# Attention of a three-stage kernel with channels on the partitions, fp32 products, and the triangular solve over pairs of chunks in PSUM

## Chip, cores and metric

The kernel runs on one core of one Trainium2 chip. The metric is device microseconds of one launch of the whole kernel.

## What is computed

The output of a linear attention with a decaying state goes through a top-1 mixture of experts and then through a gated MLP. The attention is the part that the change touches:

```
B, H, S, D = 4, 8, 768, 40
for t in range(S):
    kt, vt, rt = (k[:, :, t], v[:, :, t], r[:, :, t])
    wt, at, bt = (w[:, :, t], a[:, :, t], b[:, :, t])
    y[:, :, t] = np.einsum('bhd,bhde->bhe', rt, state)
    Sa = np.einsum('bhde,bhe->bhd', state, at)
    state_decay = state * wt[:, :, None, :] - np.einsum('bhd,bhe->bhde', Sa, bt)
    state = state_decay + np.einsum('bhd,bhe->bhde', vt, kt)
x = y in rows of tokens, 3072 x 320
# experts: of the tokens with x @ w_skip > 0, each through its best of 8 experts
out[tokens] = x + gate * (relu(x @ w1[e]) @ w2[e])
# second MLP, d_ff = 2048
h = x @ w_in; g = h * sigmoid(1.702 * h); result = g @ w_out
```

All inputs and outputs are float32.

## The kernel before

**Stages.** Attention works in 12 chunks of 64 tokens, all 32 heads at a time. The router's logits follow each half of a chunk's output; then come routing, the eight experts in groups of at most 240 tokens, and the second MLP in 6 blocks of 512 tokens. The first loads and casts of the MLPs' weights run beside attention.

**One chunk of attention.** Tokens lie on the partitions when the chunk is loaded (two batches of 64). The method `g_prep` takes the running products of the decays w by two scans on VectorE (L244, L256), one in each direction from the middle of a half chunk, and has TensorE transpose them (L269). `g_a` and `g_kb` multiply a, k and b with them on POOL (L303, L340), split the fp32 results into an fp16 high part and an fp16 rest (ScalarE's cast, POOL's subtraction), and have the DMA queue of SP transpose the parts. `g_scale` moves decays from chunk to chunk by 160 small fp32 matmuls (L204).

`g_gram` takes the products of a with k and b inside 32-token blocks (L373), transposes them into the tile Z (L385) and inverts the triangular blocks: the matrix starts as ones on the diagonal in the SBUF tile Tm, and 31 steps of two VectorE instructions follow, L396 (a column of Tm by a row of Z into tmp) and L399 (tmp added to Tm):

```
tmp[:, :n * st]   = Tm[:, r0:, st] * Z3[:, st, 0:st]        # L396, SBUF and SBUF
Tm[:, r0:, 0:st]  = Tm[:, r0:, 0:st] + tmp                  # L399, SBUF and SBUF
```

The inverse is split into fp16 parts and taken by four DMAs into the block-diagonal tile te. `g_ag` and `g_ab` make the masked products of a with k (L434, L440; fp16 rest by POOL at L451) and of a with b (L472, L480). `g_chain` solves for u of a chunk, half the heads at a time: it gathers the right side in PSUM (slots gx0, gx1), multiplies by te (L593), by the a-b products and by te again, with each vector split into parts at L585; an identity matmul (L589) takes the part that was cast out of the PSUM sum. Then it updates the state (L648 and on) and splits that. `g_sn`, `g_vt` and `g_r` bring the state, u and r into the other orientation by DMA. `g_pq` (L738, mask at L741) and `g_post` (L763 and L766, with L772) make the output; L763 is an fp32 product, of two column halves one after the other.

**Order.** Each method is a generator that yields its steps with planned costs. `weave` merges them: the step that can start first by the planned times of the engines goes next, with due times from the list RANK. What comes out is a fixed order for each engine's queue. PSUM has slots: 3 of kind c, 3 of kind g, two for gx; a step that wants one waits for it. `g_warm` puts filler matmuls (L792) on TensorE where its plan has gaps, 840 of them.

Of the kernel before, what the change touches and what calls it, by code (L numbers as in the profile page):

```python
# [23 lines left out]
def host_attn(r, k, v, w, a, b):  # L24
    B, H_, S, D_ = r.shape
    NC = S // L

    def nat(z):
        return z.reshape(2, 2, H, NC, L, D).transpose(3, 1, 4, 0, 2, 5).reshape(NC, 128, 640)

    def five(z):
        return z.reshape(2, 2, H, NC, L, D)

    k5, b5 = five(k), five(b)
    kb = np.empty((NC, 2, L, 2, 2, H, D), np.float32)
# [69 lines left out]
class Attn(Flow):  # L105
# [14 lines left out]
    def __init__(self, tc, ctx, args, NC, emit_x):  # L120
# [49 lines left out]
        for t in [st0] + self.S:  # L170
            nc.gpsimd.memset(t, 0.0)
# [1548 lines left out]
```

## Time and profile before

| | |
|---|---|
| median of 3 runs | 1163.12 us (1162.36 to 1168.79) |
| span of the profiled execution | 1164.9 us |
| busy: TensorE, VectorE | 929.5 us (80%), 797.7 us (68%) |
| busy: ScalarE, POOL | 497.2 us (43%), 473.1 us (41%) |
| mean granted TensorE clock | 0.833 of full speed |
| DMA | 140 MB in 301,625 packets |

The busy times are of one profiled execution, over all its stages; they don't say which engine ends a stage. The granted clock has two levels, 1.0 (2.4 GHz) and 0.5 (1.2 GHz); a mean between them is a mixture. A row `out<-in` names the tile that is written and those that are read, and the number after x is a count.

### The profile page before, as it was taken

What the parts mean: (1) busy time and instruction counts of PE and PEld (TensorE: products, weight loads), DVE (VectorE), ACT (ScalarE), POOL (GpSimd) and SP (SyncE); (2) the same over time, 40 slices, a digit from 0 to 9 for tenths busy, and PEclk for the clock granted to TensorE, in tenths of its full rate; (3) what the DMA queues carried; (4) which work ended last, traced back from release to release, by engine and by line L of the source; (5) the groups of instructions that cost most, each with busy time, mean ns of one, the idle gap of its engine ahead of it and who ended that gap; (6) DMA issues with size and microseconds to landing.
All of it is one profiled execution on the core that took longest, in us unless ns stands there. A gap on an engine that the chain in (4) does not pass through costs nothing.

```text
span 1164.9 us, 27321 instructions
## 1 busy us (share of the span) xinstructions
PE 929.5 (80%) x11343; PEld 654.4 (56%) x11343; DVE 797.7 (68%) x1655; ACT 497.2 (43%) x987; POOL 473.1 (41%) x405
## 2 busy tenths in 40 slices
PE   5757788598787877968840298995979999999998
PEld 5647667486566675756640176672335555555556
DVE  6599999999999999988658986766972111121110
ACT  2324555445544545436424456442543332333330
POOL 4343345435455544445313635442443332333330
PEclk8776777776777786689855599997989999999999
DMA  6564589799889798865796687434300101010000
GB/s 174 138 152 81 102 169 180 166 160 169 194 154 175 147 186 136 187 111 107 132 258 176 225 192 214 152 130 113 94 26 12 28 22 37 12 29 13 12 12 31
DMA packets 301625, 140.08 MB, mean 120 GB/s; under 512 B 271652, under 2 KB 284712, under 8 KB 299432
## 3 DMA queue, kind: packets, MB, share of 16 engines
q1 hardware_dynamic: 299192, 133.91, 52.8%
q0 software_dynamic: 2304, 4.36, 1.3%
q8 instruction: 91, 1.49, 0.5%
q14 instruction: 38, 0.31, 0.1%
HBM read 62.18 MB, written 14.48 MB: 66 GB/s over the span
## 4 chain that ended last, share of the span: by engine, by line
DVE 37%; PE 37%; DMA 11%; issue 7%; POOL 3%; ACT 3%; SPq 2%; POOLq 0%; DVEq 0%; ACTq 0%
DVE tmp L396 8%; DVE Tm L399 8%; PE c L1552 5%; PE c L1553 4%; PE c L1554 4%; PE g L1512 4%; PE g L1515 3%; PE gx L1512 3%; DMA w2s<-w 3%; PE gx L1515 2%; PE g L763 2%; PE gx L792 2%; DVE pq L741 2%; DMA d_s<-wia 1%; DMA g_x<-xd,g_ig 1%
## 5 line engine op out<-in xcount | busy, mean ns | idle before, releaser
L1535 POOL TENSOR_TENSOR glo<-g,ghi 128x512 f16<-128x512 f32 x96 | 113.8, 1187 | 221.9 <-ACT ghi L1534 221.8
L396 DVE SCALAR_TENSOR_TENSOR tmp<-Tm,Z 128x78 f32<-128x78 f32 (+21 forms) x372 | 148.9, 410 | 8.6 <-ACT Tm L383 3.0
L399 DVE TENSOR_TENSOR Tm<-Tm,tmp 128x78 f32<-128x78 f32 (+21 forms) x372 | 146.7, 405 | 5.1
L792 PE MATMUL gx<-c 128*128 128x192 f16 x840 | 131.6, 300 | 6.4 <-DMA c<-c 3.5
L1531 DVE SCALAR_TENSOR_TENSOR g<-g,sg 128x512 f32<-128x512 f32 x57 | 39.2, 688 | 133.3 <-ACT sg L1529 133.3
L1552 PE MATMUL c<-wo_hi,ghi 128*128 128x320 f16 x384 | 115.9, 302 | 5.9 <-ACT wo_hi L1457 5.9
L1553 PE MATMUL c<-wo_lo,ghi 128*128 128x320 f16 x384 | 115.1, 300 | 0.9 <-DVE wo_lo L1460 0.9
L1554 PE MATMUL c<-wo_hi,glo 128*128 128x320 f16 x384 | 115.2, 300 | 0.0
L792 PEld LDWEIGHTS <-c 128*128 128x128 f16 x840 | 82.0, 116 | 39.5 <-issue 30.1
L1534 ACT CAST ghi<-g 128x512 f16<-128x512 f32 x96 | 59.2, 618 | 76.1 <-DVE g L1531 76.1
L1531 DVE SCALAR_TENSOR_TENSOR g<-gx,sg 128x512 f32<-128x512 f32 x39 | 26.9, 689 | 89.9 <-ACT sg L1529 89.9
L451 POOL TENSOR_TENSOR gkl<-m,gkh 64x512 f16<-64x512 f32 x48 | 58.5, 1218 | 58.7 <-ACT gkh L449 46.4
L1512 PEld LDWEIGHTS <-wi_hi 128*128 128x128 f16 x480 | 45.6, 99 | 60.2 <-DMA xt<-xe 13.3
L763 PE MATMUL g<-km,pq 128*64 128x40 f32 x768 | 58.1, 261 | 26.2 <-DVE pq L741 26.1
L1512 PE MATMUL g<-xt,wi_hi 128*128 128x512 f16 x285 | 71.5, 382 | 1.3 <-DVE g L1531 1.3
L763 PEld LDWEIGHTS g<-km,pq 128*64 128x64 f32 x768 | 54.9, 172 | 29.4 <-DVE pq L741 28.4
L1515 PEld LDWEIGHTS <-wi_lo 128*128 128x128 f16 (+1 forms) x288 | 27.8, 97 | 64.1 <-issue 41.6
L1529 ACT ACTIVATE sg<-g 128x512 f32<-128x512 f32 x57 | 33.7, 595 | 64.2 <-PE g L1515 64.2
L1198 POOL TENSOR_TENSOR w2l<-w2s,w2h 128x1280 f16<-128x1280 f32 x16 | 42.9, 2687 | 44.2 <-ACT w2h L1196 44.0
L1512 PE MATMUL gx<-xt,wi_hi 128*128 128x512 f16 x195 | 49.6, 386 | 12.9 <-DMA xt<-xe 12.9
L1552 PEld LDWEIGHTS <-ghi 128*128 128x128 f16 x384 | 37.5, 98 | 28.6 <-issue 16.1
L1515 PE MATMUL g<-xt,wi_lo 128*128 128x512 f16 x171 | 52.1, 382 | 0.0
(215 smaller groups left out, 2340.6 us busy)
## 6 DMA issues: line engine op xcount, KB each, us to landing
w2s<-w SPq DMA_DIRECT2D x8, 1280.0 KB, 8.6
w1s<-w1a SPq DMA_DIRECT2D x8, 1024.0 KB, 9.4
km<-raw SPq DMA_DIRECT2D x12, 640.0 KB, 4.7
wt<-wt SPq DMA_DIRECT2D x11, 640.0 KB, 5.7
d_s<-wo SPq DMA_DIRECT2D x10, 512.0 KB, 3.6
d_s<-wia SPq DMA_DIRECT2D x8, 512.0 KB, 4.7
v<-rv SPq DMA_DIRECT2D x12, 320.0 KB, 4.2
am<-raw SPq DMA_DIRECT2D x12, 320.0 KB, 5.5
```

Of the source, the lines that this page charges most:

```text
L396: nc.vector.scalar_tensor_tensor(out=tv, in0=Tm[:, r0:, st:st + 1].to_broadcast([128, n, st]), scalar=-2.0 ** -18, in1=Z3[:, st:st + 1, 0: ...
L399: nc.vector.tensor_tensor(out=Tm[:, r0:, 0:st], in0=Tm[:, r0:, 0:st], in1=tv, op=ALU.add)
L763: mm(d, lhsT=self.pq[:, q], rhs=km[:, 40 * p:40 * p + 40], start=h == 0, stop=False, **kw)
L792: self.nc.tensor.matmul(self.X[:, 320:], lhsT=self.C['c_i'][:, 0], rhs=self.C['c_rep'].rearrange('p a b -> p (a b)')[:, :192], start=first ...
L1512: nc.tensor.matmul(h, lhsT=self.whi[:, k % 3, fs], rhs=xt[:, k], start=k == 0, stop=False)
L1515: nc.tensor.matmul(h, lhsT=self.wlo[:p, k, fs], rhs=xt[:p, k], start=False, stop=k == 2)
L1531: nc.vector.scalar_tensor_tensor(out=g, in0=h, scalar=2.0 ** -6, in1=sg2, op0=ALU.mult, op1=ALU.mult)
L1534: nc.scalar.copy(out=ghi[:, f], in_=g)
L1535: nc.gpsimd.tensor_tensor(out=glo[:, f], in0=g, in1=ghi[:, f], op=ALU.subtract)
L1552: nc.tensor.matmul(o, lhsT=ghi[:, f, s], rhs=self.ohi[:, f], start=f == 0, stop=False)
L1553: nc.tensor.matmul(o, lhsT=ghi[:, f, s], rhs=self.olo[:, f], start=False, stop=False)
L1554: nc.tensor.matmul(o, lhsT=glo[:, f, s], rhs=self.ohi[:, f], start=False, stop=f == 15)
```

## The change

**Layout.** The host lays out a, k, b, r and the decays with channels on the partitions, 40 of each 64 partitions for one half of the batch. The scans run on 128 x 1024 tiles, and a, k and b are multiplied in place by POOL; the results go straight into matmuls. A new `g_f` has TensorE transpose the decays that the output needs, and `g_kb` the products with k and b (tile km).

**Products.** All of attention's matmuls are fp32. The fp16 parts with their casts, subtractions and copies are gone, and so are all transposing DMAs in attention, the 24 DMAs that swap partition halves (FK), and `g_scale` with its 160 matmuls (11 small VectorE products instead). TensorE does the transposes, 54 of fp32 tiles a chunk, which ScalarE takes out of PSUM. The state update is a method of its own, `g_state`. The logits are fp32 as well.

**Solve.** The triangular blocks of two chunks are inverted together, in a PSUM tile of two banks that two fp16 matmuls fill with the starting values; 6 x 31 x 2 VectorE instructions on twice the elements take the place of 12 x 31 x 2. The products that follow go over heads in the outer loop and the two column halves in the inner one.

**Slots and order.** PSUM has 4 slots of kind g, no c, gx0, gx1 and the solve's two banks; after attention those two banks become c0 and c1, so that the MLPs have 6 g and 2 c (5 and 3 before). RANK has new numbers, and there are 430 filler matmuls (L628 now). The MLPs' own code is unchanged but for that.

```diff
-    SLOTS = dict(c=3, g=3, s=1, m=1, v=1, x=1)
...
+    SLOTS = dict(g=4, c=0)
...
+    def g_a(self, c):
+
+        yield ('W', c)
+        yield ('lat', c)
+        t = self.at[c % 3].rearrange('p a b c -> p (a b c)')
+        yield 'G2.4'
+        self.nc.gpsimd.tensor_tensor(out=t, in0=t, in1=self.ch[c]['W'][:, 0], op=ALU.mult)
+        self.mark('as', c)
...
+        for q in range(2):
+            yield 'G2.4'
+            t = kbT[:, 4 * q:4 * q + 4].rearrange('p a b (e t) -> p (a b) e t', e=2)
+            w = W[:, 4 * q:4 * q + 4].rearrange('p a b t -> p (a b) t').unsqueeze(2).to_broadcast([128, 8, 2, 64])
+            nc.gpsimd.tensor_tensor(out=t, in0=t, in1=w, op=ALU.mult)
+        self.mark('kb', c)
...
+                for h in range(4):
+                    nc.tensor.transpose(out=ps[:, 128 * h:128 * h + 128], in_=kbT[:, 4 * q + h, par], identity=self.C['c_id'])
+                yield 'A.33'
+                nc.scalar.copy(out=km[:, :, par, 4 * q:4 * q + 4].rearrange('p b h d -> p h b d'),
+                               in_=ps.rearrange('p (h b d) -> p h b d', h=4, b=2)[:, :, :, :40])
...
-        nc.gpsimd.memset(Tm, 0.0)
...
+        Tm = self.pt.tile([128, 2, 16, 32], F32, name='tm')
         for i in range(2):
-            nc.scalar.copy(out=flat[:, i:i + 15 * 34 + 1:34], in_=self.C['c_t0'][:, i:i + 1].to_broadcast([128, 16]))
...
-        tmp = self.tile([128, 512], F32, 'tmp', 2)
+            mm(Tm[:, i].rearrange('p a b -> p (a b)'), lhsT=self.C['c_i'], rhs=self.C['c_tm'], start=True, stop=True)
+        tmp = self.tile([128, 272], F32, 'tmp')
         for st in range(31, 0, -1):
             r0 = st // 2
             n = 16 - r0
-            tv = tmp[:, :n * st].rearrange('p (a b) -> p a b', b=st)
-            d = f'D{.07 + n * st / 960}'
+            tv = tmp[:, :2 * n * st].rearrange('p (q a b) -> p q a b', q=2, b=st)
+            d = f'D{.06 + 2 * n * st / 960}'
             yield d
-            nc.vector.scalar_tensor_tensor(out=tv, in0=Tm[:, r0:, st:st + 1].to_broadcast([128, n, st]), scalar=-2.0 ** -18,
-                                           in1=Z3[:, st:st + 1, 0:st].to_broadcast([128, n, st]), op0=ALU.mult, op1=ALU.mult)
+            nc.vector.tensor_tensor(out=tv, in0=Tm[:, :, r0:, st:st + 1].to_broadcast([128, 2, n, st]),
+                                    in1=Z4[:, :, st:st + 1, 0:st].to_broadcast([128, 2, n, st]), op=ALU.mult)
             yield d
-            nc.vector.tensor_tensor(out=Tm[:, r0:, 0:st], in0=Tm[:, r0:, 0:st], in1=tv, op=ALU.add)
...
+            nc.vector.tensor_tensor(out=Tm[:, :, r0:, 0:st], in0=Tm[:, :, r0:, 0:st], in1=tv, op=ALU.subtract)
```


The solve's products and the state:

```diff
         def times(z, w, t, start=False):
-            for h in range(8):
-                mm(z[:, 40 * h:40 * h + 40], lhsT=w[:, hb * 8 + h], rhs=t[:, h], start=start and h == 0, stop=True, **kw)
-        yield 'A.35'
-        xh = part('xh', X, -2.0 ** -12)
-        yield '+c'
+            w = w.rearrange('p (a u) t -> p a u t', a=2)
+            for h, par, p, d, o in both:
+                mm(z[o, d], lhsT=w[:, par, hb * 8 + h], rhs=t[:, h], start=start and h == 0, stop=True, **kw)
+        yield 'A.33'
+        x = part('x', X, -1.0)
+        yield '+g'
...
-        yield 'P.55*.96'
-        add(X, id12, xh)
+        yield 'P.95*1.3'
         U = self.pst(sc)
-        times(U, teh, xh, True)
-        times(U, tel, xh)
-        yield 'A.35'
-        xl = part('xl', X, -2.0 ** -12)
-        yield 'P.21*.32'
-        times(U, teh, xl)
-        yield 'A.35'
-        uh = part('uh', U, 2.0 ** -6)
-        yield 'P.55*.96'
-        add(U, id6, uh)
-        times(X, bh, uh, True)
-        times(X, bl, uh)
-        yield 'A.35'
-        ul = part('ul', U, 2.0 ** -6)
-        yield 'P.35*.64'
-        times(X, bh, ul)
+        times(U, self.tz, x, True)
...
+        times(U, self.tz, x)
...
+    def g_state(self, c):
...
+            mm(ps, lhsT=self.C['c_id'], rhs=ST[:, 8 * par:8 * par + 8].rearrange('p a b -> p (a b)'), start=True, stop=False, **kw)
+            for h in range(8):
+                for hb in range(2):
+                    p = hb * 16 + par * 8 + h
+                    mm(ps[64 * hb:64 * hb + 40, 40 * h:40 * h + 40], lhsT=km[:, p], rhs=vu[:, p], start=False, stop=True, **kw)
...
-        for par in range(2):
-            for h in range(8):
-                p, q = hb * 16 + par * 8 + h, par * 8 + h
+        for h in range(8):
+            for par in range(2):
                 d = Y[64 * par:64 * par + 64, 40 * h:40 * h + 40]
-                mm(d, lhsT=self.pq[:, q], rhs=km[:, 40 * p:40 * p + 40], start=h == 0, stop=False, **kw)
-        for par in range(2):
-            for h in range(8):
-                mm(Y[64 * par:64 * par + 64, 40 * h:40 * h + 40], lhsT=rT[:120, hb * 8 + h, 64 * par:64 * par + 64],
-                   rhs=S[:120, h, 64 * par:64 * par + 40], start=False, stop=True, **kw)
+                e = 64 * (h % 2)
+                mm(d, lhsT=self.pq[0][:, 4 * par + h // 2, e:e + 64], rhs=km[:, hb, par, h], start=h == 0, stop=False, **kw)
...
+                more = actx.enter_context(tc.tile_pool(name='b_ps', bufs=1, space=PS))
+                A.ps = Banks(A.ps, c0=more, c1=more)
```


In VectorE's queue, early in attention: before, the elimination steps of two chunks stand in turn (tmp and Tm are one chunk's tiles).

```order
L396 SCALAR_TENSOR_TENSOR tmp<-Tm,Z 128x96
L396 SCALAR_TENSOR_TENSOR tmp<-Tm,Z 128x58
L399 TENSOR_TENSOR Tm<-Tm,tmp 128x12x8
L399 TENSOR_TENSOR Tm<-Tm,tmp 128x2x29
L396 SCALAR_TENSOR_TENSOR tmp<-Tm,Z 128x91
L396 SCALAR_TENSOR_TENSOR tmp<-Tm,Z 128x56
L399 TENSOR_TENSOR Tm<-Tm,tmp 128x13x7
L399 TENSOR_TENSOR Tm<-Tm,tmp 128x2x28
L396 SCALAR_TENSOR_TENSOR tmp<-Tm,Z 128x78
L396 SCALAR_TENSOR_TENSOR tmp<-Tm,Z 128x81
```

Now each row works on both chunks of a pair; L212 is a scan of a later chunk's decays.

```order
L336 TENSOR_TENSOR tmp<-tm,Z 128x200
L339 TENSOR_TENSOR tm<-tm,tmp 128x2x4x25
L336 TENSOR_TENSOR tmp<-tm,Z 128x192
L339 TENSOR_TENSOR tm<-tm,tmp 128x2x4x24
L336 TENSOR_TENSOR tmp<-tm,Z 128x230
L212 SCALAR_TENSOR_TENSOR W<-wt,c_d_90 128x1024
L339 TENSOR_TENSOR tm<-tm,tmp 128x2x5x23
L215 TENSOR_TENSOR tots<-W,wt 128x32
L336 TENSOR_TENSOR tmp<-tm,Z 128x220
L219 RECIPROCAL tot<-tots 128x32
```

The steps are half as many, with the same shapes twice over (2 x 5 x 23 for 5 x 23), and tm lies in PSUM.

In TensorE's queue, in the solve of a chunk: before, part by part (xl, uh and ul are fp16 parts, boh the a-b products, c_81 an identity, L792 fillers).

```order
L593 MATMUL c_1342<-xl_1365,te 128x40
L792 LDWEIGHTS c_81
L792 MATMUL gx_814<-c_81 128x192
...
L589 LDWEIGHTS c_81
L589 MATMUL c_1316<-uh_1390,c_81 128x320
L593 LDWEIGHTS boh
L593 MATMUL gx_814<-uh_1390,boh 128x40
```

Now the second chunk's solve, both halves of the heads in turn: tz is the inverse, bz the a-b products, x and y the vectors, km and vu the state's operands; a row with x16 is sixteen products.

```order
L462 MATMUL g_1398<-x_1390,tz 64x40 x16
L462 MATMUL g_1415<-x_1396,tz 64x40 x16
L462 MATMUL gx_528<-y_1432,bz_111 64x40 x16
L462 MATMUL gx_549<-y_1450,bz_111 64x40 x16
L462 MATMUL g_1398<-x_1473,tz 64x40 x16
L462 MATMUL g_1415<-x_1494,tz 64x40 x16
L441 MATMUL gx_1519<-vu,m_799 64x40 x16
L441 MATMUL gx_1546<-vu,m_806 64x40 x16
L506 MATMUL g_1565<-ST,c_86 128x320
L510 MATMUL g_1565<-vu,km 40x40 x16
L556 MATMUL g_1588<-c_86,vu 80x128 x4
```

The extra products for the parts and the identity matmuls are gone; between the solve's products stand the state's (L506, L510), transposes (L556) and the next chunk's products of a with k (L371).

## Rows read from the trace of the kernel before

**Rows 1.** The page, busy time of each engine and share of the span.

```profile
PE 929.5 (80%) x11343; PEld 654.4 (56%) x11343; DVE 797.7 (68%) x1655; ACT 497.2 (43%) x987; POOL 473.1 (41%) x405
```

**Rows 2.** Windows: length, busy us of PE, PEld, DVE, ACT, POOL, granted clock, DMA.

```profile
100.00:150.00 50.00, 41.94 (x780) 35.16 (x780) 47.50 (x118) 27.83 (x68) 19.01 (x16) 0.74 0.62 113
300.00:350.00 50.00, 38.05 (x695) 30.32 (x695) 49.23 (x116) 24.30 (x58) 27.39 (x24) 0.75 0.83 163
600.00:650.00 50.00, 11.00 (x156) 10.13 (x156) 41.45 (x87) 20.14 (x27) 15.48 (x8) 0.50 0.73 222
666.00:700.00 34.00, 34.00 (x259) 25.01 (x258) 30.00 (x61) 19.32 (x27) 13.38 (x10) 1.00 0.85 219
800.00:1164.00 364.00, 346.01 (x1920) 180.33 (x1920) 108.28 (x151) 128.95 (x225) 113.82 (x96) 0.98 0.12 33
```

**Rows 3.** The page, the chain that ended last, by line.

```profile
DVE tmp L396 8%; DVE Tm L399 8%; PE c L1552 5%; PE c L1553 4%; PE c L1554 4%; PE g L1512 4%; PE g L1515 3%; PE gx L1512 3%; DMA w2s<-w 3%; PE gx L1515 2%; PE g L763 2%; PE gx L792 2%; DVE pq L741 2%; DMA d_s<-wia 1%; DMA g_x<-xd,g_ig 1%
```

**Rows 4.** The page's groups of the elimination, and its first line by source.

```profile
L396 DVE SCALAR_TENSOR_TENSOR tmp<-Tm,Z 128x78 f32<-128x78 f32 (+21 forms) x372 | 148.9, 410 | 8.6 <-ACT Tm L383 3.0
L399 DVE TENSOR_TENSOR Tm<-Tm,tmp 128x78 f32<-128x78 f32 (+21 forms) x372 | 146.7, 405 | 5.1
...
L396 DVE SCALAR_TENSOR_TENSOR tmp<-Tm,Z x372: 155/264/2933, 48.1 to 561.4; 128x126 f32<-128x126 f32 x18, 128x56 f32<-128x56 f32 x13, 128x78 f32<-128x78 f32 x13, 128x96 f32<-128x96 f32 x13
```

**Rows 5.** Timeline of VectorE and POOL: start, us, engine, line, operation, tiles, shape.

```profile
201.53 1.50 DVE L399 TENSOR_TENSOR Tm<-Tm,tmp 128x110 f32<-128x110 f32 x1
203.06 0.27 DVE L396 SCALAR_TENSOR_TENSOR tmp<-Tm,Z 128x108 f32<-128x108 f32 x1
...
201.34 1.57 POOL L303 TENSOR_TENSOR am<-am,F 128x640 f32<-128x640 f32 x1
202.84 0.53 POOL L380 MEMSET Tm<- 128x512 f32 x1
```

**Rows 6.** The same two engines, 279 to 281 us.

```profile
279.13 0.68 DVE L741 TENSOR_TENSOR pq<-g,c 128x512 f32<-128x512 f32 x1
279.73 0.89 DVE L399 TENSOR_TENSOR Tm<-Tm,tmp 128x130 f32<-128x130 f32 x1
...
279.01 1.47 POOL L314 TENSOR_TENSOR sm<-am,sm 128x640 f16<-128x640 f32 x1 [0.18 <-DVE kbs L345]
```

**Rows 7.** L741 and L244 by source (ns min/median/max), L1531 from the page.

```profile
L741 DVE TENSOR_TENSOR pq<-g,c x48: 647/680/692, 143.1 to 606.9; 128x512 f32<-128x512 f32 x48
L1531 DVE SCALAR_TENSOR_TENSOR g<-g,sg 128x512 f32<-128x512 f32 x57 | 39.2, 688 | 133.3 <-ACT sg L1529 133.3
L244 DVE TENSOR_TENSOR_SCAN wt<-wt,c_d x12: 1474/1482/2684, 7.2 to 416.1; 128x640 f32<-128x640 f32 x12
```

**Rows 8.** Timeline of TensorE at the output products, clock 1.0, then 0.5.

```profile
153.79 1.68 PE L763 MATMUL g<-km,pq 128*64 128x40 f32 x29
155.24 0.21 PE L766 MATMUL g<-S,rT 120*64 120x40 f16 x1
...
155.35 0.23 PE L763 MATMUL g<-km,pq 128*64 128x40 f32 x1
155.41 0.23 PE L763 MATMUL g<-km,pq 128*64 128x40 f32 x1
...
190.74 2.92 PE L763 MATMUL g<-km,pq 128*64 128x40 f32 x29
```

**Rows 9.** Timeline of TensorE: transposes at 0.5 and 1.0, Gram products, fillers.

```profile
100.85 0.85 PE L269 MATMUL g<-c,wt 128*128 128x128 f32 x3
...
250.96 0.49 PE L269 MATMUL g<-c,wt 128*128 128x128 f32 x3
...
155.81 1.35 PE L373 MATMUL g<-aT,kbt 120*32 120x32 f16 x57
...
118.86 0.49 PE L792 MATMUL gx<-c 128*128 128x192 f16 x4
```

**Rows 10.** ScalarE's router logits by source, with the first and last start.

```profile
L998 ACT ACTIVATE lg<-g x24: 150/178/185, 159.8 to 625.3; 128x9 f32<-128x9 f32 x24
```

More of the change, by code (lines that the diff above doesn't have):

```diff
@@ L129, in __init__ @@
         self.C = {}
-        self.ch = {0: {}}
+        self.ch = {c: {} for c in range(NC)}
+        F = lambda n: n in self.EARLY
+        new = lambda shape, dt, name: (self.pe if F(name) else self.cst).tile(shape, dt, name=name)
+        self.wt = new([128, 2, 1024], F32, 'wt')
+        nc.vector.memset(self.wt, 1.0)
+        for q, i in ((0, 0), (1, 31)):
+            nc.vector.memset(self.wt[:, q].rearrange('p (a s) -> p a s', s=32)[:, :, i:i + 1], 0.0)
         for n, d in (('c_32', F32), ('c_16', F16)):
@@ new lines, in __init__ @@
+        self.kbT = [new([128, 8, 2, 128], F32, f'kbT{i}') for i in range(2)]
+        self.rT = [new([80, 2, 16, 64], F32, f'rT{i}') for i in range(2)]
+        for t in self.at + self.kbT + self.rT:
+            nc.gpsimd.memset(t, 0.0)
+        self.tz, *self.bz = self.zero = [new([128, 32, 64], F32, n) for n in ('tz', 'bz0', 'bz1')]
+        self.pq = [self.cst.tile([128, 8, 128], F32, name='pq')]
+        self.tot = self.cst.tile([128, NC, 16, 2], F32, name='tots')
+        self.scl = self.cst.tile([128, NC, 16], F32, name='scl')
@@ L214, in load @@
-    def load(self, n, c):
-        a, w = self.args, dict(wt=1280, am=640, km=1280)[n]
-        src = dict(wt=lambda: a['wt'][c].rearrange('q p a b -> p q (a b)'), am=lambda: a['raw'][c, :, :640],
-                   km=lambda: a['raw'][c, :, 640:])[n]()
-        t = self.tile([128, w], F32, n, self.KM if n == 'km' else 1)
-        t = t.rearrange('p (q x) -> p q x', q=2) if n == 'wt' else t
-        for q in range(2) if n == 'wt' and not c else (slice(None), ):
-            self.nc.sync.dma_start(out=t[:, q], in_=src[:, q])
-        self.ch.setdefault(c, {})[n] = t
@@ new lines, in g_v @@
+        yield ('Sx', c - 2)
+        yield 'Q.6>E3.2'
+        vu = self.tile([128, 32, 40], F32, 'vu', 2)
+        self.nc.sync.dma_start(out=vu.rearrange('p a x -> p (a x)'), in_=self.args['rv'][c])
+        self.ch[c]['vu'] = vu
+        self.mark('v', c)
+    def g_r(self, c):
+        yield ('Y', c - 2)
+        for e in range(2):
+            yield 'Q.6>E.8'
+            self.nc.sync.dma_start(out=self.rT[c % 2][40 * e:40 * e + 40, e].rearrange('p a b -> p (a b)'), in_=self.args['rT'][c, e])
@@ new lines, in g_sn @@
+    def g_sn(self, c):
+        nc = self.nc
+        yield ('S', c)
+        yield ('Y0', c)
+        yield ('Y1', c)
+        S = self.S = self.tile([80, 8, 128], F32, 'S')
+        ST = self.state[c + 1].rearrange('p a b -> p (a b)')
+        for par in range(2):
+            yield '+g'
+            sg = self.got
+            yield 'P.44*.5'
+            ps = self.pst(sg)[:80]
+            for j in range(4):
+                o = 320 * par + 80 * j
+                nc.tensor.transpose(out=ps[:, 128 * j:128 * j + 128], in_=ST[:, o:o + 80], identity=self.C['c_id'])
+            yield 'A.51'
+            nc.scalar.copy(out=S[:, 4 * par:4 * par + 4].rearrange('p a b -> p (a b)'), in_=ps)
+            self.give(sg)
+        self.mark('vs', c)
+        self.mark('Sn', c)
```

863 lines of the change are left out of this document (303 added, 560 removed), and 24 rows, old and new, of the table RANK.

## The prediction

> **What bounds the kernel now.** I read the page's engine totals and slices first, then windows of 50 us, the chain that ended last, and last the instructions of the places that the chain names. TensorE is busy 80% of the span and VectorE 68% [rows 1], but that is an average over two programs. The windows part them [rows 2]: in two stretches of attention VectorE is busy 47.5 and 49.2 of 50 us, while TensorE, filler matmuls (L792) included, has 42 and 38 at a granted clock of 0.74 and 0.75; after 800 us TensorE has 346 of 364 at 0.98 and VectorE 108. So attention is VectorE's and the experts and the second MLP are TensorE's. The chain agrees: the two lines of the elimination, L396 and L399, come first in it with 8% each [rows 3]. They are 744 instructions and 295.6 us of VectorE [rows 4].
>
> Why do they cost 0.40 us each? Take 200.8 to 205.1 us [rows 5]. L396 on 108 elements a partition takes 0.27; L399 on 110 takes 1.50, and it began 0.19 us after POOL's L303, a 1.57 us product of two SBUF tiles. A memset on POOL at 202.84 stretches nothing: the L396 at 203.06 is the 0.27. So an elimination step whose two inputs lie in SBUF waits for a POOL product beside it. The other kind is at 279 us [rows 6]: L741 reads PSUM and SBUF, POOL's L314 runs all through it, and it takes 0.68, as all 48 of them do (647 to 692 ns [rows 7]); the L399 behind it, under the same POOL instruction, takes 0.89.
>
> The Trainium skill ("SBUF — State Buffer", "Who interferes with whom") states this as a rule: a VectorE instruction with two SBUF inputs and a GpSimd one that reads SBUF exclude each other, and one with at most one SBUF input does not contend. Rows 5 and 6 agree.
>
> **The change, part by part.**
>
> VectorE. The triangular matrix now lies in PSUM, so each step has one SBUF input. Unstretched, a step costs about 0.155 us, the least of L396 [rows 4], plus 1.04 ns an element (0.27 at 108 [rows 5], 0.68 at 512 [rows 6]). In pairs of chunks there are 372 steps with the same elements in all, 24 x 2856: 372 x 0.155 + 71 = 129 us for 295.6. Writing to PSUM is in no row; a PSUM source costs nothing at 512 elements (680 ns in L741 against 688 in L1531, whose sources lie in SBUF [rows 7]), so I take 0, with 0 to 0.1 us a step (0 to 37 us) as bounds. The other work per chunk: two scans of 1024 elements, 2 x 1.48 x 1024/640 = 4.7; pq and m, 6 x 0.68 = 4.1 [rows 7]; transposes, state, output and routing some 5.7, by like instructions. With 10.8 of elimination VectorE has 25 us per chunk, where a chunk took 42.8 (513 us over 12, [rows 4]). Copies, casts and subtractions into fp16 parts leave ScalarE with the evacuations alone, and POOL with products of some 4400 elements a chunk, 10.7 us at L303's 1.57 for 640 [rows 5]. The 94 transposing DMAs and the 24 half swaps leave SP's queue, and all that waited behind them comes earlier.
>
> TensorE. It gives up fp16 parts and takes fp32, and I make it the new bound. The terms per chunk, at full clock and at half:
> - 16 groups of 16 products with 64 weight columns and 40 moving ones (10 in the solve, 4 in the output, 2 in the state). In L763, two passes a product, a pass follows the last after 0.06 us at full clock, and 29 of the 32 passes span 1.68 us, or 2.92 at half [rows 8]. There one half of the columns comes first and then the other. The changed code alternates them. If they then run side by side, 16 passes set a group: 0.93, or 1.62 at half by the same ratio. The seam speaks for it: 32 passes 58 ns apart would take 1.80 from first to last start, and they took 1.62 (153.79 to 155.41), and L766 starts in the other half while L763 still issues. I take 14.9 and 25.9; bounds 26.9 and 46.7 without any overlap beyond that seam.
> - 54 fp32 transposes at 0.11 or 0.21 (three L269 in 0.49 and 0.85 [rows 9]): 5.9 and 11.5. 16 full-width products for pq, two passes each: 3.5 and 6.8.
> - The small Gram products, 96 of two passes at 21 ns (57 L373 in 1.35 us [rows 9]): 4.0 and 4.8. The products for m, 64 passes spaced between those of L373 and L763, 0.04 and 0.073: 2.6 and 4.7. State carry, logits, filling the PSUM matrix by the same spacings: 2.0 and 3.6.
> - 240 filler matmuls between the first solve and the end, 21 a chunk at 0.08 (0.49 us for 4 [rows 9]) or 0.16: 1.7 and 3.3.
>
> The sum is T = 34.6 us per chunk at full clock and 60.6 at half. The clock decides between them, and what the rows show of it is: VectorE as the bound and TensorE waiting goes with 0.75; 600 to 650, almost no matmuls, with 0.50; 666 to 700, where TensorE is busy all 34 us, with 1.00 [rows 2]. With TensorE as the bound it should lie nearer to the last; but a chunk is some 45 short groups that wait for evacuations, so not at it. I take full clock for three quarters of the time: 1 / (0.75/34.6 + 0.25/60.6) = 39 us.
>
> Start and end. Today the first elimination step is at 48.1 us [rows 4]. A pair needs two chunks prepared: two more scans (4.7) and one more turn of POOL's products (10.7), against four transposing and swapping DMAs of 3 to 7 us that leave the way; I keep 45 us. Then 21.5 us for 62 steps and 2.6 for the way out: the first solve at 69 us. By then about a third of a chunk of TensorE's work is done, so 11.67 are left. After the last logits (625.3 us [rows 10]) the code is the same but for one PSUM slot moved from c to g: 1164.9 - 625.3 = 540 us; for the slot I take 0, bounds -10 to +10.
>
> Sum: 69 + 11.67 x 39 + 540 = 1064 us of span. The span of before is 1.8 us above the median of its runs, so 1062.
>
> **The rivals.**
>
> *The column halves do not run side by side.* Then a group costs 1.68 or 2.92, T is 34.6 + 12 = 46.6 at full clock, 81 at half and 52 at my clock, and the time is 69 + 11.67 x 52 + 540 = 1216, or 1153 with a full clock. This is the slower side, and it decides from T = 47.6, where the sum is 1164.9. For it: L763 took 1.68, not 0.93. Against it: the seam and L766.
>
> The Trainium skill ("TensorE: Matmul & The Clock Gate", Part 3) says a weight load overlaps matmuls in flight only where the row group differs, and two column halves share theirs; by that rule this rival is the case. The seam [rows 8] speaks against the rule.
>
> *The clock stays where it is, 0.75.* T = 1/(0.5/34.6 + 0.5/60.6) = 44 and 1123 us: the upper end of my forecast. At half clock throughout, T = 60.6 gives 1316.
>
> *TensorE keeps waiting, for slots or for VectorE.* There are four g slots. Some 30 uses a chunk, 0.95 to fill and 0.6 to empty, take 30 x 1.55 / 4 = 12 us; they bind only if each evacuation waits over 3.6 us. VectorE's queue is in order, and a pq product there stands between elimination steps and 2.4 us scans. With half of that wait on the path T is 44 to 47: 1125 to 1155.
>
> *The stretching stays.* If PSUM did not free the steps from POOL, they could lose at most POOL's 10.7 us per chunk: VectorE has 36, still under 39. The forecast does not hang on it; fewer POOL products alone would do.
>
> *All fits and the clock is full.* T = 34.6: 1013 us, less with a better start.
>
> **Chances.** TensorE as the bound at a clock of 0.75 to 1.0, 1013 to 1123: 0.62, with 1062 as its middle. Faster still, through products cheaper than my rows: 0.10. Waits that leave 1123 to 1157: 0.11. Within 0.5%, which is about what a measurement of this kernel can tell from no change: 0.04. Slower, through column halves one after the other or a low clock: 0.13. The range 990 to 1155 leaves out the slower cases and the few below.
>
> **What would show it.** Right: VectorE busy some 25 us per chunk in the windows of attention, L336 and L339 near 0.35 us each with no long ones, TensorE over 45 of 50, a solve group in about 1 us at full clock, the last logits near 525. Wrong: groups of 1.7 us; TensorE idle while g slots are full; a clock of 0.75 or less; the first solve well after 69 us; or a stage after attention that no longer takes 540.

## The result, and the profile after

The changed kernel takes 1128.59 us (median of 4 runs, 1113.78 to 1150.53) beside 1165.38 for the kernel before (1162.36 to 1168.79): a ratio of 0.957 (0.954 to 0.961). The two later pairs of the same two kernels gave 0.974 (0.968 to 0.979) and 0.957 (0.954 to 0.960). Over its 14 executions the changed kernel takes 1113.8 to 1150.5 us, with 1133 in the middle, and the time goes with the mean granted clock: 0.88 in the shortest, 0.854 in the longest. The ratios compare the less disturbed executions of each kernel, the medians all of them. So the gain is some 30 to 50 us. The forecast was 103: the sign was right and the time lies within the range, but the size is less than half.

Which step lost it? The rows below are of the execution of 1127.8 us (span 1125.9), the one nearest to the middle. First its page: engine totals, the chain that ended last by engine, and the two lines of the elimination, which answer to [rows 1], [rows 3] and [rows 4].

```profile
PE 1010.9 (90%) x13633; PEld 758.5 (67%) x13633; DVE 584.0 (52%) x1070; ACT 394.6 (35%) x780; POOL 365.0 (32%) x277
...
PE 62%; DVE 16%; issue 7%; DMA 7%; POOL 5%; ACT 2%; SPq 1%; POOLq 0%; DVEq 0%; ACTq 0%
...
L339 DVE TENSOR_TENSOR tm<-tm,tmp 128x252 f32<-128x252 f32 (+22 forms) x186 | 66.0, 355 | 4.8
L336 DVE TENSOR_TENSOR tmp<-tm,Z 128x252 f32<-128x252 f32 (+22 forms) x186 | 64.3, 346 | 4.9
```

TensorE is now 62% of the chain and VectorE 16%. The elimination takes 64.3 + 66.0 = 130.3 us in place of 295.6. Now a window of the kernel before and then four of the changed one (columns as in [rows 2]).

```profile
108.00:625.00 517.00, 392.46 (x7648) 323.98 (x7648) 469.65 (x1118) 253.30 (x581) 234.68 (x211) 0.74 0.82 159
```

```profile
117.00:591.00 474.00, 457.03 (x9363) 414.25 (x9362) 262.85 (x578) 165.20 (x406) 116.19 (x99) 0.82 0.29 81
134.00:182.00 48.00, 48.00 (x701) 44.40 (x697) 17.52 (x42) 13.34 (x34) 8.22 (x7) 0.53 0.20 56
182.00:236.00 54.00, 52.95 (x1315) 47.11 (x1315) 30.15 (x39) 20.33 (x53) 14.49 (x12) 0.98 0.34 98
800.00:1125.00 325.00, 316.32 (x1801) 169.56 (x1800) 78.51 (x109) 112.05 (x197) 100.54 (x86) 0.99 0.09 24
```

Between the first solve and the last logits VectorE was busy 470 of 517 us; now TensorE is, with 457 of 474, and VectorE has 263, which is 22.5 a chunk (forecast 25). That is the step from one bound to the other, as forecast. The clock in this stretch is 0.82: 0.53 from 134 to 182 us and 0.98 in the next 54, with TensorE as busy in both. The stages behind it stayed TensorE's, 316 of 325 us at 0.99 after 800.

Where the stretches begin and end: the solve (L462) and the logits (L846) of the changed kernel by source, and below them the solve (L593) of the kernel before.

```profile
L462 PE MATMUL g<-x,tz x1536: 196/229/329, 117.1 to 559.7; 128*64 128x40 f32 x192
...
L846 ACT ACTIVATE lg<-g x24: 168/179/189, 171.0 to 591.4; 128x9 f32<-128x9 f32 x24
```

```profile
L593 PE MATMUL c<-xh,te x768: 179/201/241, 107.9 to 582.6; 128*128 128x40 f16 x192
```

With these three rows the account closes:

| stretch | before | changed | measured | forecast |
|---|---|---|---|---|
| start to the first product with the inverse | 107.9 | 117.1 | +9 | -39 (to 69) |
| from there to the last logits | 517.4 | 474.3 | -43 | -62 |
| after the last logits | 539.6 | 534.5 | -5 | 0 |
| span | 1164.9 | 1125.9 | -39 | -101 |

Two terms failed: the start by 48 us and the pace by 19.

**The start.** VectorE from the first scan to the first elimination step, and at that elimination's end (timeline of the changed kernel):

```profile
23.17 2.29 DVE L212 TENSOR_TENSOR_SCAN W<-wt,c_d 128x1024 f32<-128x1024 f32 x1 [13.52 <-DMA rT<-rT]
...
27.30 2.29 DVE L225 TENSOR_TENSOR_SCAN W<-wt,c_d 128x1024 f32<-128x1024 f32 x1
...
38.49 2.33 DVE L212 TENSOR_TENSOR_SCAN W<-wt,c_d 128x1024 f32<-128x1024 f32 x1 [8.82 <-DMA wt<-wt]
...
55.99 4.48 DVE L212 TENSOR_TENSOR_SCAN W<-wt,c_d 128x1024 f32<-128x1024 f32 x1 [4.51 <-DMA wt<-wt]
...
67.72 1.97 DVE L322 STREAM_TRANSPOSE Z<-Za 128x1024 f32<-128x1024 f32 x1 [3.19 <-ACT Za L315]
...
71.42 0.21 DVE L336 TENSOR_TENSOR tmp<-tm,Z 128x62 f32<-128x62 f32 x1
...
111.22 1.04 DVE L345 STREAM_TRANSPOSE Tc<-tm 128x512 f32<-128x512 f32 x1
112.12 1.82 DVE L322 STREAM_TRANSPOSE Z<-Za 128x1024 f32<-128x1024 f32 x1
113.87 1.01 DVE L345 STREAM_TRANSPOSE Tc<-tm 128x512 f32<-128x512 f32 x1
```

The first step comes at 71.4, not 45. The first scan waits 13.5 us for loads and starts at 23.2, where it started at 7.2 in the kernel before [rows 7]; the second chunk's scan waits another 8.8 for `wt`. SyncE's queue tells why: two of its waits, summed up to 117 us, and its issues around 11, 30 and 47 us.

```profile
SPq L195 <- DVE W L225: 14.2, 2, 10.6
...
SPq L422 <- POOL rT L157: 8.7, 2, 7.2
```

```profile
10.87 2.03 SPq L422 DMA_DIRECT2D rT<-rT  x2
...
15.03 0.36 SPq L195 DMA_DIRECT2D wt<-wt  x1
...
29.62 0.28 SPq L195 DMA_DIRECT2D wt<-wt  x1
29.94 0.33 SPq L195 DMA_DIRECT2D kbT<-kbT  x1
...
46.78 0.28 SPq L195 DMA_DIRECT2D wt<-wt  x1
47.11 0.33 SPq L195 DMA_DIRECT2D kbT<-kbT  x1
```

There is one `wt` buffer. The load of the next chunk's decays waits until VectorE has ended the second scan (27.30 + 2.29 = 29.6), and the load of `kbT` stands behind it in the same queue. Ahead of that, the loads of `rT` wait for POOL to clear their buffers, and the first chunk's second half of `wt` stands behind them: it is issued at 15.0, and the scan that needs it starts 8.1 us later.

Then 62 steps take 71.4 to 111.2, 39.8 us where 21.5 were forecast: the scans and transposes for the next chunks (at 77, 83, 95 and 103 us among others) stand between them in VectorE's queue. Two transposes into Tc (111.22 and 113.87) have another chunk's Z between them. Last, TensorE (timeline), which waits 11.5 us for the second Tc: L328, which fills the PSUM matrix for the next pair, stands ahead of the first solve in its queue.

```profile
102.14 1.33 PE L628 MATMUL gx<-c 128*128 128x192 f16 x14
114.93 1.01 PE L328 MATMUL tm<-c 128*128 128x512 f16 x2 [11.46 <-DVE Tc L345]
115.73 1.48 PE L628 MATMUL gx<-c 128*128 128x192 f16 x8
117.15 1.55 PE L462 MATMUL g<-x,tz 128*64 128x40 f32 x32
```

So the 48 us are four pieces: the first scan 16 us later than before, 48.2 us from it to the first step where the 45 left 37.8 (10), the steps (18), and the way out, 5.9 us for 2.6 (3).

**The pace.** The solve's groups, TensorE's timeline at clock 1.0 and then at 0.5:

```profile
301.18 1.13 PE L462 MATMUL g<-x,tz 128*64 128x40 f32 x32
302.24 0.66 PE L286 MATMUL g<-c,kbT 128*128 128x128 f32 x4
...
307.30 1.11 PE L441 MATMUL gx<-vu,m 128*64 128x40 f32 x32
308.23 1.11 PE L462 MATMUL g<-x,tz 128*64 128x40 f32 x32
...
448.19 3.64 PE L462 MATMUL g<-x,tz 128*64 128x40 f32 x64
451.63 1.17 PE L462 MATMUL gx<-y,bz 128*64 128x40 f32 x18
```

From start to next start, 32 passes take 0.93 us in front of a group of their own kind and 1.06 in front of L286; at half clock, 3.44 / 2 = 1.72. The forecast had 0.93 and 1.62 for 16 passes in each half, side by side. The column halves pair. The sum of the terms holds too: the formula of the prediction with the clock that was measured, 0.82, gives 1 / (0.64/34.6 + 0.36/60.6) = 40.9 us a chunk, and 474.3 / 11.67 = 40.6 was measured. In eight profiles, three of this kernel and five of variants below that only change the start, the clock is 0.78 to 0.87 and a chunk takes 42.3 to 38.2 us, and the formula comes out 0.3 to 0.8 us high. What failed is the clock, taken as 0.875.

### The profile page after: what moved, and what is told of

Its sections match the earlier page's. It is cut to its first block, busy times and chain, and to the rows that moved or that the text cites. A ratio compares the mean times of both kernels' runs of the same rounds, so it can differ in the third digit from the quotient of the medians.

```text
span 1148.7 us, 30697 instructions
## 1 busy us (share of the span) xinstructions
PE 1028.9 (90%) x13633; PEld 776.2 (68%) x13633; DVE 586.3 (51%) x1070; ACT 394.8 (34%) x780; POOL 365.2 (32%) x277
## 3 DMA queue, kind: packets, MB, share of 16 engines
q8 instruction: 109, 1.79, 0.6%
## 4 chain that ended last, share of the span: by engine, by line
PE 63%; DVE 15%; DMA 8%; issue 8%; POOL 3%; ACT 1%; SPq 1%; POOLq 0%; DVEq 0%; ACTq 0%
PE g L1360 5%; PE c L1400 5%; PE g L462 4%; PE c L1401 4%; PE c L1402 4%; PE g L575 4%; PE g L1363 3%; PE gx L441 3%; PE g L371 2%; PE g L556 2%; PE gx L1360 2%; PE g L603 2%; PE gx L462 2%; PE gx L448 2%; DMA w2s<-w 2%
## 5 line engine op out<-in xcount | busy, mean ns | idle before, releaser
L813 POOL TENSOR_TENSOR xr<-xo,xr 128x256 f16<-128x256 f32 (+1 forms) x44 | 24.5, 578 | 179.3 <-ACT xr L809 179.3
L275 POOL TENSOR_TENSOR kbT<-kbT,W 128x1024 f32<-128x1024 f32 x24 | 62.2, 2608 | 57.9 <-DMA kbT<-kbT 40.4
L462 PE MATMUL g<-x,tz 128*64 128x40 f32 x1536 | 68.9, 262 | 0.7 <-issue 0.6
L339 DVE TENSOR_TENSOR tm<-tm,tmp 128x252 f32<-128x252 f32 (+22 forms) x186 | 66.0, 355 | 4.9
L462 PEld LDWEIGHTS g<-x,tz 128*64 128x64 f32 x1536 | 64.5, 175 | 4.4 <-issue 2.6
L336 DVE TENSOR_TENSOR tmp<-tm,Z 128x252 f32<-128x252 f32 (+22 forms) x186 | 64.4, 346 | 4.9
L575 PE MATMUL g<-rT,vt 80*128 80x128 f32 x384 | 66.6, 334 | 0.0
L575 PEld LDWEIGHTS g<-rT,vt 80*128 80x128 f32 x384 | 59.2, 239 | 1.5
L1363 PE MATMUL g<-xt,wi_lo 128*128 128x512 f16 (+1 forms) x192 | 59.6, 388 | 0.0
L577 DVE TENSOR_TENSOR pq<-g,c 128x512 f32<-128x512 f32 x48 | 32.9, 686 | 49.9 <-PE g L575 49.8
```

The costliest lines, as they stand in the source:

```text
L275: nc.gpsimd.tensor_tensor(out=t, in0=t, in1=w, op=ALU.mult)
L336: nc.vector.tensor_tensor(out=tv, in0=Tm[:, :, r0:, st:st + 1].to_broadcast([128, 2, n, st]), in1=Z4[:, :, st:st + 1, 0:st].to_broadcast([ ...
L339: nc.vector.tensor_tensor(out=Tm[:, :, r0:, 0:st], in0=Tm[:, :, r0:, 0:st], in1=tv, op=ALU.subtract)
L462: mm(z[o, d], lhsT=w[:, par, hb * 8 + h], rhs=t[:, h], start=start and h == 0, stop=True, **kw)
L575: nc.tensor.matmul(ps[:, 128 * j:128 * j + 128].rearrange('p (e t) -> p e t', e=2), lhsT=vt[:, i], rhs=rT[:, :, i], start=True, stop=True)
L1363: nc.tensor.matmul(h, lhsT=self.wlo[:p, k, fs], rhs=xt[:p, k], start=False, stop=k == 2)
```

## Experiments

Two names stand in what was expected: "first solve" is the first start of the product with the inverse, and T is the time from there to the last logits over 11.67.

**The changed kernel again.** No edit; it runs beside the experiments of its group.

> The changed kernel again, unchanged, for a profile beside those of the other runs. The theory from its first profile: TensorE is the bound from the first solve on (busy 476 of 493 us), at the pace forecast, and what the forecast missed is the start: first solve at 119 us, not 69. So here: first solve (first product with tz) at 115 to 120, last logits at 575 to 615, the rest 535 to 540, TensorE busy over 47 of 50 us in between. The rival, that the pace was missed, wants over 42 us per chunk between first solve and last logits at a mean granted clock near 0.85.

1132.42 us (1127.81 to 1138.78), the rows above. Beside the later groups:

> The changed kernel again, for a median on the same chip as the three runs beside it: 1125 to 1140 us, first solve at 117 to 119.

1134.93 us (1114.24 to 1143.55); in its profile the first solve at 115.8, T 41.3, clock 0.80. The start repeats within 2 us; the mean clock of the stretch was 0.78 in the profile of the first group, 0.82 in the one shown above, and 0.80 here.

**Does the start pass through?** About 20 us of VectorE work ahead of the first elimination:

```diff
         tmp = self.tile([128, 272], F32, 'tmp')
+        if not c0:
+            for _ in range(60):
+                nc.vector.memset(tmp, 0.0)
```

> 60 extra small memsets on VectorE ahead of the first pair's elimination, about 20 us, nothing else in any queue moved. If the late first solve costs its full length (theory A), the time grows by 17 to 22 us. If the limit is TensorE's total work, and it does other work while it waits for the first solve (theory B: it was busy 45.7 of 50 us from 50 to 100 already), the time grows by 0 to 6.

1153.51 us (1150.49 to 1172.19), 21 above the changed kernel of the same group. First solve 138.7 (+21.6), T 41.0. A later start passes through one to one. Whether an earlier one comes back in full is another question, which the next runs ask.

**Two buffers for the decays, and `rT` cleared by VectorE.** (The tile scl gives up a chunk's row that nothing reads, for room.)

```diff
-        wt = self.wt
+        wt = self.wts[c % 2]
...
-        for t in self.at + self.kbT + self.rT:
+        for t in self.rT:
+            nc.vector.memset(t, 0.0)
+        for t in self.at + self.kbT:
             nc.gpsimd.memset(t, 0.0)
```

> A second buffer for the decays' tile wt, so that a chunk's load no longer waits for the scans of the chunk before, and what stands behind it in SP's queue (the second half of kbT) no longer waits either; the rT tiles are cleared by VectorE instead of POOL. The order of every queue is otherwise kept. The first solve should come at 95 to 105 instead of 119. Theory A: the time falls by as much, 14 to 24 us. Theory B: by under 6.

1119.46 us (1102.76 to 1143.92). First solve 110.7: 6 earlier, not 12 to 22. The first scan starts at 20.1 instead of 23.2 and the first step comes at 66.6 instead of 71.4, so most of the late start is not the one `wt` buffer. Run again with more executions:

> The kernel of e2b_start again, on the same chip as the changed kernel. Its first solve was 6.4 us earlier: the time is 4 to 10 us under the changed kernel's.

1109.36 us (1087.8 to 1146.36), 0.940 of the kernel before (0.936 to 0.944), first solve 111.7, T 38.6, clock 0.86. The mean of the ten executions with two buffers is 1115.9, of the changed kernel's 14 it is 1131.2: 15 us (give or take 7), and the ratios of this group, 0.940 and 0.957, lie 20 us apart. The earlier start would give 4 to 6, so there is probably more to it. Here is a stretch in which the profiles differ: first this run, then the other two profiles of the changed kernel, and last the gap ahead of this run's first solve.

```profile
134.00:168.00 34.00, 33.64 (x774) 30.38 (x770) 18.11 (x42) 14.19 (x37) 8.86 (x7) 1.00 0.38 107
```

```profile
134.00:182.00 48.00, 48.00 (x710) 44.14 (x707) 19.48 (x47) 11.56 (x29) 6.22 (x5) 0.50 0.19 52
134.00:182.00 48.00, 48.00 (x686) 44.07 (x684) 16.92 (x40) 13.91 (x35) 8.89 (x7) 0.54 0.22 61
```

```profile
109.49 1.01 PE L331 MATMUL tm<-c 128*128 128x512 f16 x2 [8.96 <-DVE Tc L348]
```

From the second chunk's solve to the third's it is 34.4 us (134.3 to 168.7); in the changed kernel it was 52.2 (138.2 to 190.4). In both TensorE is busy with hardly a break, 33.64 of 34 us here and 48.00 of 48 there; the clock is 1.00 here and 0.53 there. This repeats: all three profiles of the changed kernel have 0.50 to 0.54 from 134 to 182 us, and both profiles with two buffers have 1.00. Why it does is not shown: TensorE idles ahead of the first solve in both kernels, 9.0 us here and 11.5 there.

**The elimination kept in order at the start.** On the kernel with two buffers, the scans of the fourth and fifth chunk wait for the first pair:

```diff
         yield ('kb', c - 2)
+        if c in (3, 4):
+            yield ('elim', 0)
```

> The start of e2b_start, and the scans of chunks 3 and 4 are planned behind the first pair's elimination instead of between its steps. The first elimination should take 25 us from first to last step instead of 38, the first solve come at 95 to 100 us. If the start passes to the end in full, the time is 10 to 15 us under e2b_start and 20 to 25 under the changed kernel; if TensorE then runs out of prepared chunks, since chunks 3 and 4 come later, the gap comes back as TensorE idle time before the third or fifth chunk, and the time is that of e2b_start.

First solve 100.8, about as expected: the steps run from 65.9 to 90.9, 24.9 us, so 15 of the 39.8 were the work between them. But the time is 1127.05 us (1106.33 to 1143.48), no gain over two buffers alone: in its profile T rose to 41.9 at a clock of 0.80, and from the last logits to the first expert product it is 46 us (589.4 to 635.4) where the changed kernel has 33. In POOL's queue a split of the experts' weights (w2l, 620.2 to 622.8) now stands ahead of the gather of their rows (g_x), which starts at 623.0 and started at 612.5 in the changed kernel. So a start 16 us earlier than the changed kernel's brought nothing back at the end; that rests on one profile and four executions.

**Most of the first pair's steps left out** (the last 28 of 31, so the inverse of that pair is not formed):

```diff
+            gone = not c0 and st < 29
-            nc.vector.tensor_tensor(out=tv, in0=Tm[:, :, r0:, st:st + 1].to_broadcast([128, 2, n, st]),
+            gone or nc.vector.tensor_tensor(out=tv, in0=Tm[:, :, r0:, st:st + 1].to_broadcast([128, 2, n, st]),
...
-            nc.vector.tensor_tensor(out=Tm[:, :, r0:, 0:st], in0=Tm[:, :, r0:, 0:st], in1=tv, op=ALU.subtract)
+            gone or nc.vector.tensor_tensor(out=Tm[:, :, r0:, 0:st], in0=Tm[:, :, r0:, 0:st], in1=tv, op=ALU.subtract)
```

> Left out: the last 28 of the 31 steps of the first pair's elimination (its inverse is then not the inverse); every queue keeps its order. What is left between are the scans of chunks 3 and 4 and their loads, so the first solve should come 14 to 18 us earlier, at 99 to 103. If the start passes to the end (as 20 us of delay did), the time falls by 12 to 20 us; if TensorE's other work is the limit before that, by under 6. With the scans gone as well it would be 26.

1107.68 us (1092.42 to 1148.38) beside 1134.93; means 16 apart, give or take 11. First solve 107.1, 9 us earlier and not 14 to 18. The time agrees with the start's price and is too loose to measure it.

**One column half after the other** in the solve, the products for m, the state and the output; the same products in another order:

```diff
-        for h in range(8):
-            for par in range(2):
+        for par in range(2):
+            for h in range(8):
```

> The solve's, the state's and the output's products and those for m go through one column half and then the other, as in the kernel before; same products, same places in the queue otherwise. If the alternation is what makes 16 passes set a group (the forecast's term of 0.93 us), a group goes from about 0.9 to about 1.7 us at full clock, TensorE has 12 us per chunk more, and the time grows by 100 to 170 us. If the engine pairs the halves whatever the order, or never does, it changes by under 15.

1330.31 us (1305.45 to 1333.83): +198 between the medians, +178 between the shortest executions, more than expected. Its groups, clock 1.0 and then 0.5:

```profile
399.75 1.85 PE L462 MATMUL g<-x,tz 128*64 128x40 f32 x32
401.54 0.66 PE L286 MATMUL g<-c,kbT 128*128 128x128 f32 x4
...
425.74 3.23 PE L462 MATMUL g<-x,tz 128*64 128x40 f32 x32
428.90 1.33 PE L371 MATMUL g<-at,kbT 64*64 64x64 f32 x10
```

1.79 us for 32 passes in front of L286 where alternating took 1.06, and 3.16 for 1.72. This rival was real, and the order of two loops decides it. Its T by the prediction's formula at this run's clock of 0.74 (half of the time at each level) is 1 / (0.48/46.6 + 0.52/81) = 60; 57.1 was measured.

The Trainium skill ("TensorE: Matmul & The Clock Gate", Part 3) lets a weight load overlap matmuls in flight only where the row group differs. The halves use the same rows, and 1.06 against 1.79 us speaks against that rule for these products.

**The elimination in SBUF again**, all else as changed: ScalarE copies the pair's matrix into an SBUF tile first.

```diff
+        tS = self.tile([128, 2, 16, 32], F32, 'tS')
+        nc.scalar.copy(out=tS.rearrange('p q a b -> p (q a b)'), in_=Tm.rearrange('p q a b -> p (q a b)'))
+        Tm = tS
```

> The pair's triangular matrix is copied by ScalarE from PSUM to an SBUF tile and eliminated there, so that each step reads SBUF twice as in the kernel before; all else and the order are kept. If attention is TensorE's now, only the first elimination stands on the path: the steps' sum grows by 20 to 60 us (those beside a POOL product are stretched to a microsecond or more), first solve 3 to 10 us later, the time 0 to 12 us longer. If taking the steps out of POOL's way is itself what gained, the time goes back toward the kernel before, by 25 us or more.

1161.82 us (1141.21 to 1183.91), 0.985 of the kernel before (0.980 to 0.990). The two lines by source, of this kernel and then of the changed one:

```profile
L339 DVE TENSOR_TENSOR tmp<-tS,Z x186: 155/376/3184, 72.9 to 555.8; 128x252 f32<-128x252 f32 x18, 128x60 f32<-128x60 f32 x12, 128x112 f32<-128x112 f32 x12, 128x156 f32<-128x156 f32 x12
...
L342 DVE TENSOR_TENSOR tS<-tS,tmp x186: 197/383/2462, 74.5 to 556.0; 128x252 f32<-128x252 f32 x18, 128x60 f32<-128x60 f32 x12, 128x112 f32<-128x112 f32 x12, 128x156 f32<-128x156 f32 x12
```

```profile
L336 DVE TENSOR_TENSOR tmp<-tm,Z x186: 151/366/442, 71.4 to 510.7; 128x252 f32<-128x252 f32 x18, 128x60 f32<-128x60 f32 x12, 128x112 f32<-128x112 f32 x12, 128x156 f32<-128x156 f32 x12
...
L339 DVE TENSOR_TENSOR tm<-tm,tmp x186: 190/372/450, 71.7 to 510.9; 128x252 f32<-128x252 f32 x18, 128x60 f32<-128x60 f32 x12, 128x112 f32<-128x112 f32 x12, 128x156 f32<-128x156 f32 x12
```

The medians are alike; the longest are 3184 and 2462 ns for 442 and 450. In PSUM no step is stretched by POOL, in SBUF some are, as the Trainium skill has it ("SBUF — State Buffer", "Who interferes with whom"). All that adds only 28 us of VectorE time (77.9 + 80.7 for 130.3), yet the time rises by 29 us between the medians, and the ratios, 0.985 beside 0.957 to 0.974, say 13 to 33. The prediction called stretched steps harmless; they are not. How they cost it the trace shows only in part. In the window from the first solve to the last logits

```profile
123.00:636.00 513.00, 486.95 (x9362) 440.68 (x9362) 284.40 (x580) 169.64 (x411) 116.28 (x99) 0.77 0.27 75
```

TensorE idles 26 us for 17, and the first solve is 6 us later (123.3). The rest of this profile's extra time is the same products at a clock of 0.77 instead of 0.82, and one profile of the changed kernel had 0.78 without any stretched step.

**Is VectorE off the path at all?** Two memsets behind each step from the second pair on, 10 us a chunk:

```diff
+            if c0:
+                nc.vector.memset(tmp, 0.0)
+                nc.vector.memset(tmp, 0.0)
```

> From the second pair on, two more small memsets on VectorE behind every elimination step, about 0.34 us each, 21 us per pair or 10 per chunk. If VectorE is off the path (25 us of work in 40), the time grows by under 6 us. If its in-order queue still sets the pace, it grows by 40 us or more.

1218.88 us (1210.73 to 1224.32): +86, with VectorE busy 82 us more in the stretch (345 for 263). The longest of TensorE's waits between the first solve and the end of attention, and the window of the pace:

```profile
PE g L601 <- DVE tm L339: 13.7, 1, 13.7
PE g L509 <- DVE ST L517: 11.6, 5, 5.0
PE g L837 <- DVE xo L612: 6.8, 2, 6.4
```

```profile
119.00:671.00 552.00, 497.71 (x9304) 447.85 (x9302) 345.30 (x882) 165.26 (x404) 114.20 (x99) 0.74 0.25 70
```

VectorE is busy 63% here and still costs that much: it works through its queue in order, so a small piece that TensorE wants (the new state ST, the output xo) stands behind steps. Against the changed kernel TensorE idles 37 us more (54 for 17) and is busy 41 us more (498 for 457) on the same products, at a clock of 0.74 for 0.82. So about half comes as waits and half as a lower clock; why the clock fell is not shown.

**Can the clock be held?** Three fillers of 192 columns behind each group of the solve, 18 a chunk:

```diff
+            for i in range(3):
+                mm(z[:, 320:], lhsT=self.C['c_i'], rhs=self.C['c_tm'][:, :192], start=False, stop=True, **kw)
```

> Three filler matmuls of 192 columns behind each of the six groups with tz and bz in a chunk's solve, 18 a chunk. The granted clock in attention was 0.82 although TensorE was busy 96% of it. If the short fp32 products are what lets the clock fall, the fillers bring it to 0.9 or more, T goes from 40.6 to 37 to 39, and the time falls by 15 to 40 us. If not, they cost their own 0.08 to 0.16 us each, 1.4 to 2.9 a chunk, and the time grows by 15 to 35.

1152.61 us (1143 to 1179.05); T 42.8, clock 0.82 as without them. They cost their own time and do not lift it.

Then 130 fillers in the one long gap before the first solve, ahead of L328, on the changed kernel and on the one with two buffers:

```diff
+        for i in range(130 if c0 == 2 else 0):
+            mm(self.X[:, 320:], lhsT=self.C['c_i'], rhs=self.C['c_tm'][:, :192], start=False, stop=True, skip_group_check=True)
```

> The changed kernel with 130 more filler matmuls in TensorE's queue just ahead of the refill of the solve's PSUM tile for the second pair, where TensorE stood idle from 103.5 to 114.9 us waiting for VectorE. They cost 0.08 us each at full clock, 10 us of that idle time. In the changed kernel the clock was 0.5 at 107 to 117 us and again from 131 to 179, with TensorE busy all 48 us of it. If the idle time at the first solve is what puts that stretch at half clock, the third chunk's solve comes 10 to 20 us earlier (at 170 to 178 instead of 189) and the time falls by 10 to 25. If dense fp32 products let the clock fall by themselves, nothing changes beyond 5 us.

> The same fillers in the kernel with two wt buffers (e12_wt2). Where the clock was already 1.0 from 128 to 241 us there, little is left to gain: 0 to 10 us under e12_wt2, 1095 to 1110.

On the changed kernel 1140.83 us (1115.18 to 1156.2): no gain, where 10 to 25 us were expected if the gap decides. In its profile the third solve is at 169.6, as expected, and the stretch that had 0.53 reads:

```profile
134.00:168.00 34.00, 33.64 (x800) 30.56 (x798) 19.01 (x44) 13.81 (x36) 8.86 (x7) 1.00 0.36 99
```

So that stretch was won, and the profiled execution is the shortest of the six (1115.18), but the executions together are no faster than without the fillers: one stretch's level decides too little. With two buffers it is 1101.86 us (1095.04 to 1138.57), 0.941 of the kernel before (0.9375 to 0.945): the same as without the fillers.

**Fewer products on TensorE.** 14 of each 16 products of pq with km left out, so the output and with it the logits are others:

```diff
-                mm(d, lhsT=self.pq[0][:, 4 * par + h // 2, e:e + 64], rhs=km[:, hb, par, h], start=h == 0, stop=False, **kw)
+                if h == 0:
+                    mm(d, lhsT=self.pq[0][:, 4 * par + h // 2, e:e + 64], rhs=km[:, hb, par, h], start=True, stop=False, **kw)
```

> Left out: 14 of the 16 products of pq with km in each half of the output (L598), so 28 products a chunk, 1.6 us at full clock and 2.9 at half; nothing waits for less or more otherwise. If TensorE's work sets the pace after the first solve, the time falls by 20 to 30 us. If VectorE's queue sets it (10 us more a chunk there cost 86), it falls by under 8.

```profile
118.00:574.00 456.00, 431.94 (x8693) 388.91 (x8690) 265.27 (x580) 164.45 (x407) 115.58 (x99) 0.82 0.31 85
```

At the clock of the profile above, 0.82, TensorE is busy 25 us less; 18 of them come as time (T is 39.0, 1.6 us less a chunk, where 20 to 30 us in all were expected) and 7 as waiting. So TensorE's work sets most of the pace. The whole, 1162.39 us, says nothing, since with other logits the experts' work is another, and the stretch behind the last logits took 603 us.

## Why the prediction was right and where it was wrong

- *Elimination, 129 us:* 130.3. Right. PSUM as a destination costs nothing that shows. "The stretching stays", judged harmless: wrong. The judgement was by a sum of busy time (36 under 39 us), and two runs show that VectorE at 55 to 63% busy already makes the time longer; in the one with 63% TensorE's idle time grew from 17 to 54 us, because what TensorE needs waits in VectorE's queue.
- *Column halves side by side:* right, and now shown: 1.06 against 1.79 us, and 178 to 198 us of time. It was the rival that would have made the kernel slower.
- *T at either clock:* right as a sum. Single terms were not, and cancelled: a pass of the Gram products of L312 took 11 ns for 21, a full-width one (L575) 124 for 109, an fp32 transpose (L286) 0.145 us for 0.11, and only 24 filler matmuls stand in the stretch, 2 a chunk where the sum has 21.
- *The clock, 0.875:* wrong, 0.82, which is 19 us of the 62 missed. The step that failed was to read the clock from how busy TensorE is, by the row at 666 us with 34 of 34 us at 1.00 [rows 2], and to put attention three quarters of the way there. Here is a stretch busy 48.00 of 48 us at 0.53, and the same work at 1.00 in another run. One kernel's executions differ by 37 us, and the clock goes with it. What decides the level in a given stretch stays open: fillers within the groups did not raise the mean, a filled gap went with 1.00 in one stretch and with no shorter time, and with two buffers that stretch had 1.00 without a filled gap.
- *First solve at 69:* wrong, 117, the largest miss. The working began at the first elimination step of before (48.1), kept 45, and added 24. The right row was the first product with the inverse, L593 at 107.9: it lies 60 us behind that step, where the prediction put 24. In the forecast's own terms, the 45 us to the first step were 71, the 21.5 of the steps were 39.8, and the 2.6 of the way out were 5.9. The 45 assumed that loads and first scan stay where they were. The first scan came 16 us later, with half of `wt` behind `rT` in SyncE's queue; `wt` with one buffer then waits for the scan before it, and `kbT` stands behind it. Of the steps' 18 us, 15 are scans and other work between them. The runs took back 6 us (two buffers) and 16 (with the steps kept together); what the rest of the start needs stays open.
- *After the last logits, 0:* -5, within its bounds.
- *The rivals in time:* 1128 lies where "the clock stays" and "TensorE keeps waiting" pointed. Neither is the case: the clock rose from 0.74 to 0.82, and TensorE waits only 17 of 474 us. A time that fits a rival does not show its mechanism.

The best version is the changed kernel with two `wt` buffers, 0.940 of the kernel before (0.936 to 0.944).

## What to carry to other kernels

Where a stage becomes faster, read where its first result is used today, not where its first instruction starts, and list every load that waits for a buffer on the way there. An engine that is idle over a third of the time can still cost time if it works through a queue in order: ask how long the piece that others wait for stands in it. When a bound moves to TensorE, forecast with both clock levels and don't choose between them by busy share.

## What the hardware showed that was not expected

- Two 64-column halves of fp32 products run side by side if the instructions alternate: 1.06 us for 32 passes against 1.79, at half clock 1.72 against 3.16, with the same group behind them at full clock.
- A stretch of short fp32 products with hardly a break ran at 0.50 to 0.54 in three profiles of one kernel, with TensorE busy 48.00 of 48 us, and at 1.00 in those of two variants with the same products, 33.64 of 34 us.
- A scan with two SBUF inputs is stretched like a product: L212 took 2.29 us, and 4.48 from 55.99 us on, where POOL's L275, two products of SBUF tiles, ran from 53.7 to 58.3 us.
